# Attention outputs of a linear-attention and two-layer MoE kernel: products of 128 rows against products of 64 rows in two halves of the array

## The chip, the cores and the metric

The kernel runs on one core of a Trainium2 chip. The metric is the device time of one execution in microseconds (us), smaller is better; several executions of each kernel are timed and the median is given. The core has a matrix engine (TensorE, in the profile PE for products and PEld for the loads of their stationary operand), VectorE (DVE), ScalarE (ACT), GpSimd (POOL) and SyncE (SP), which issues most of the transfers. Products write to PSUM, eight banks of 512 fp32 values in each of 128 partitions; ACT and DVE read them from there.

## The reference

Linear attention without a softmax over 8 batches, 8 heads, 576 tokens and a head size of 64, a norm over each head, and then two layers with 512 inputs, 2048 hidden units and 512 outputs over all 4608 tokens. All in fp32.

```python
kv = einsum('bhsd,bhse->bhde', k, v)              # one 64x64 matrix for each batch and head
out = einsum('bhsd,bhde->bhse', q, kv)
rms = sqrt(mean(out * out, axis=-1, keepdims=True) + 1e-06)
x = (out / rms * g_norm)                          # then (batch, token, head * 64 + e): 4608 x 512
h = x @ moe_w_in;  y = (h * sigmoid(h)) @ moe_w_out
h2 = y @ moe2_w_in; r = maximum(h2, 0); result = (s * r * r + b) @ moe2_w_out
```

## The kernel before

The tokens of a batch are cut into four tiles of 128 tokens and a rest of 64; the rests of two neighbouring batches share one tile of 128 partitions. That makes 32 full tiles and 4 rest tiles. Batch 0 is done at the start, by itself (the last part of the code); the seven others are spread over the first layer.

The first layer runs in 7 blocks of 512 tokens with 16 slots each, one slot for 128 of the hidden units. In a slot, `emit_h` (L493) issues twelve products of 128x128 by 128x512 into a bank `ph`, and ACT applies Silu. After it, `attend` (L560) issues what the list `UNITS` assigns to this slot: for a batch b, one tile of attention in each of four or five consecutive slots, and four to eight slots later the transposes of the normed tiles. The code issues in this order by hand (a manual schedule), so that on each engine the order of the code is the order of execution. The remaining layers (the classes Hidden and Output, seven products in place of eight by Strassen's and Winograd's scheme) follow and are not touched.

One tile of attention consists of these steps:

- `emit_qT` (L373), one slot earlier: four transposes of 128x128 on PE, from q into a PSUM bank `pq`, and one ACT copy of 128x512 into `qT`, which is a part of the tile `at_kvw`. There is one such room for all tiles.
- `out_tile` (L436) calls `emit_out` (L382): for each of the four pairs of heads one fp32 product, with 128 rows (two heads of 64), the transposed q of 128 tokens as stationary operand and a 128x128 matrix `kvw` as moving operand. `kvw` holds the two heads' 64x64 matrices on its diagonal and zeros elsewhere, so that one product gives both heads. All four pairs go to one PSUM bank `po`. A rest tile has two products for each pair, one for each batch, of 64 tokens each: the left and the right half of the array's columns. An fp32 product has two records of a load and two of a matmul in the trace.
- ACT squares `po` into `sq` (L395), DVE sums the squares of each head (L396), and ACT copies `po` to `xnp` or `xr` (L444). Later DVE makes the reciprocal roots (`rsqrt_steps`), multiplies (`emit_norm`, L432), and PE transposes (`emit_xT`, L464).

The banks: `pq` and `po` take turns in the two banks a_0 and a_1. `ph` has h_0 and h_1; `pkv` (the 64x64 matrices of a batch, L353 and L359) y0; the transposes `px` y2 and y3; y1 is not used beside the first layer. In the opening of batch 0, four banks y0 to y3 hold one tile each (`pss`, L1214); for pairs 0 and 1, and then for pair 2 and pair 3, the `kv` matrices and the outputs of all four tiles are made in turn, as k and v arrive, and squares, sums, norm and transposes go tile by tile.

Of the kernel before, what the change touches and what calls it, by code (L numbers as in the profile page):

```python
# [8 lines left out]
F32 = mybir.dt.float32  # L9
F32R = mybir.dt.float32r  # L10
I32 = mybir.dt.int32
AF = mybir.ActivationFunctionType
ALU = mybir.AluOpType
AX = mybir.AxisListType
# [3 lines left out]
def kernel(  # L18
# [36 lines left out]
    nc = tc.nc  # L55
    P = 128
    B, H, S, D = q.shape
    NT, DM = out.shape
    DFF = moe_w_in.shape[1]
    NP = H // 2  # L60
    KT = DM // P
    MT = DFF // P
    T = 512
    NB = NT // T
    TT = T // P
# [19 lines left out]
    ps_y = Turns(psum, 1)  # L85
# [3 lines left out]
    def room(tag, shape, dtype, name):  # L89
        return sbuf.tile(shape, dtype, tag=tag, name=name)  # L90

    def bank(tag, name):
        return psum.tile([P, T], F32, tag=tag, name=name)
# [5 lines left out]
    def pair(tag, name):  # L99

        return room(tag, [P, 2, T], F32, name)
# [4 lines left out]
    xn_pages = [pair(tag, f"xnp{i}") for i, tag in enumerate(("XA", "XB"))]  # L106
    kvw = [at_kvw[:, 1].rearrange("p (a t) -> p a t", a=NP), const.tile([P, NP, P], F32, tag="kvw1", name="kvw1")]
# [6 lines left out]
    def runs(t):  # L114
        b, c = t
        return [(0, P, b)] if c < TT else [(i * ST, ST, b - 1 + i) for i in range(2)]
# [18 lines left out]
    def load_raw(stage, i, tag):  # L135
        a = room(tag, [P, WN, 2], I32, f"wr{stage}_{i}")
        w = weights[stage].bitcast(I32)
        if stage % 2:
            nc.sync.dma_start(
                a.rearrange("p (c f) o -> p c (f o)", c=KT),  # L140
                w[:, 4 * i * P:4 * (i + 1) * P].rearrange("(c p) f -> p c f", p=P),
            )
        else:
            nc.sync.dma_start(
                a.rearrange("p (r e) o -> p r (e o)", r=2),
                w[2 * i * P:2 * (i + 1) * P, :].rearrange("(r p) e -> p r e", p=P),
            )
        raw_t[stage, i] = a
# [178 lines left out]
    qT_t = {}  # L327
    xn_t = {}
# [43 lines left out]

    def emit_qT(t):  # L373
        a = q_t.pop(t).rearrange("p h d -> p (h d)")
        ps = ps_a.tile([P, T], F32, tag="a", name=f"pq{t[0]}_{t[1]}")
        for p in range(NP):
            nc.tensor.transpose(ps[:, p * P:(p + 1) * P], a[:, p * P:(p + 1) * P], ident)  # L377
        qT = at_kvw[:, 0].rearrange("p (a t) -> p a t", a=NP)
        nc.scalar.copy(qT.rearrange("p a t -> p (a t)"), ps)
        qT_t[t] = qT  # L380

    def emit_out(t, ps, pairs):  # L382

        po = ps.rearrange("p h d -> p (h d)")
        for p in pairs:
            for off, n, b in runs(t):
                nc.tensor.matmul(  # L387
                    po[off:off + n, p * P:(p + 1) * P], qT_t[t][:, p, off:off + n], kvw[b % 2][:, p, :],
                    start=True, stop=True,
                )  # L390

    def emit_squares(t, ps, ms):

        sq = work.tile([P, H, D], F32, tag="sg", name=f"sq{t[0]}_{t[1]}", bufs=3)
        nc.scalar.activation(sq, ps, AF.Square)  # L395
        nc.vector.reduce_sum(ms, sq, axis=AX.X)  # L396

    def rsqrt_steps(r, tiles):
# [24 lines left out]
    def xn_page(t):  # L423
        if t[1] == TT:
            return room("gl_0", [P, H, D], F32, f"xr{t[0]}")
        return xn_pages[t[1] // 2][:, t[1] % 2].rearrange("p (h d) -> p h d", h=H)

    def emit_norm(t, x, y):
        xn = xn_t.get(t)
        if xn is None:  # L430
            xn = xn_t[t] = xn_page(t)
        nc.vector.tensor_tensor(xn, x, y.rearrange("p (h o) -> p h o", o=1).to_broadcast([P, H, D]), op=ALU.mult)  # L432

    r_t = {}

    def out_tile(t):  # L436
        b, i = t
        if i == 0:
            r_t[b] = small.tile([P, 4, 6 * H], F32, tag="r", name=f"r{b}", bufs=1)
        ps = ps_a.tile([P, H, D], F32, tag="a", name=f"po{b}_{i}")  # L440
        emit_out(t, ps, range(NP))
        emit_squares(t, ps, r_t[b][:, 0, i * H:(i + 1) * H])
        xn_t[t] = xn_page(t)
        nc.scalar.copy(xn_t[t], ps)  # L444

    def norm_tile(t):
        b, i = t
# [89 lines left out]
    def first_load_q(i):  # L537
        a = spare(f"W{5 + i}", f"q0_{i}").rearrange("p (h c d) -> p h c d", h=NP, c=TT)
        x = q[0, i * NP:(i + 1) * NP, :T, :]
        nc.sync.dma_start(a.rearrange("p h c d -> p h (c d)"), x.rearrange("h (p c) d -> p h (c d)", c=TT))  # L540
        return a
# [477 lines left out]
    def warm_up(n):  # L1019

        ps = ps_h.tile([P, T], F32, tag="h", name="warm")
        for _ in range(n):
            nc.tensor.matmul(ps, kvw[1][:, 0, :], kvw[1].rearrange("p a t -> p (a t)"), start=True, stop=True)
# [162 lines left out]
    with tc.manual_schedule():  # L1186
        load_raw(1, 0, "wr_0")
        qs = [first_load_q(0), first_load_q(1)]
        kvs = [first_load_kv(0), first_load_kv(1)]
        kvz = first_load_z()  # L1190
        load_raw(1, 1, "wr_1")
        kvs += [first_load_kv(2), first_load_kv(3)]
        nc.vector.memset(bcol, 0.0)
        nc.vector.memset(ones, 1.0)
        nc.scalar.activation(scol, bcol, AF.Silu)
        for t in kvw:
            nc.gpsimd.memset(t, 0.0)
        make_identity(nc, ident)
        gv = g_norm.rearrange("(d o) -> d o", o=1)
        for i in range(2):  # L1200
            nc.scalar.dma_start(gcol[i * D:(i + 1) * D], gv)
        nc.scalar.dma_start(scol, moe2_s.rearrange("(a o) -> a o", o=1).to_broadcast([P, 1]))
        nc.scalar.dma_start(bcol, moe2_b.rearrange("(a o) -> a o", o=1).to_broadcast([P, 1]))
        warm_up(4)

        def first_kv(p):
            a = kvs[p]
            kv_t[0, p] = []
            for i in range(2):
                kv_t[0, p] += [a[:, i], [kvz[:ST, i, 2 * p + h] for h in range(2)]]  # L1210
            emit_kv(0, [p])

        r = r_t[0] = small.tile([P, 4, 6 * H], F32, tag="r", name="r0", bufs=1)
        pss = [ps_y.tile([P, H, D], F32, tag=f"y{t}", name=f"po{t}") for t in range(TT)]  # L1214
        decode_first(0, "rebias", "low", "sign", "merge")
        decode_first(0, "high", "rest")
        for t in range(TT):
            first_qT(t, qs)
        first_kv(0)
        first_kv(1)  # L1220
        for t in range(TT):
            emit_out((0, t), pss[t], (0, 1))
        decode_first(1, "rebias", "low", "sign", "merge")
        load_kv(1, 0)
        load_kv(1, 1)
        for p in (2, 3):
            first_kv(p)
            for t in range(TT):
                emit_out((0, t), pss[t], (p,))
            load_kv(1, p)  # L1230
        for t in range(TT):
            emit_squares((0, t), pss[t], r[:, 0, t * H:(t + 1) * H])
        decode_first(1, "high")
        warm_up(4)
        for step in rsqrt_steps(r, range(TT)):
            step()
        for t in range(TT):
            emit_norm((0, t), pss[t], r[:, 2, t * H:(t + 1) * H])
        for t in range(TT):
            if t < 2:  # L1240
                emit_xT((0, t), ps_a.tile([P, NP, P], F32, tag="a", name=f"px0_{t}"))
            else:
                emit_xT((0, t), ps_y.tile([P, NP, P], F32, tag=f"y{t - 2}", name=f"px{t}"))
        decode_first(1, "rest")
        decode_first(2, "rebias", "low", "sign", "merge")

        def in_spares():

            kept = {}

            def granule(n):
                if n % 2 == 0:
                    kept[0] = room(SPARES[n // 2 % NA], [P, 2, 2, 2 * P], F32R, f"wo{n}")
                return kept[0][:, n % 2]

            return granule

        def in_pages(n):
            return room(("kvw1_0", "gh_0", "v_0")[n % 3], [P, 2, 2 * P], F32R, f"wp{n}")

        steps = (f for s in (
            weight_steps(2, ("wr_0", "wr_1"), ("v_0", "v_1"), in_spares(), 3, behind=3),
            weight_steps(3, ("wr_0", "wr_1"), ("v_0", "v_1"), in_spares(), 3),
        ) for f in s)
        steps4 = weight_steps(4, ("wr_1",), ("K",), in_pages, 2)
        for j in range(PB):
            for m in range(MT):
                emit_h(j, m)
                first_stage(j, m, steps)
        hidden1.run(beside1)  # L1270
        out2.run(beside2)
        hidden3.run(beside3)
        do_some(steps4, 1000)
        out4.run(beside4)
# [33 lines left out]
```

## Time and profile before

| | |
|---|---|
| median of 3 executions | 1563.76 us (1562.29 to 1566.73) |
| the profiled execution's own time | 1564.93 us |
| its span in the profile | 1562.8 us |
| PE busy | 1541.8 us, 99% of the span |
| DVE busy | 1016.7 us, 65% |
| ACT busy | 821.5 us, 53% |
| granted TensorE clock | 1.0 |

A profile shows each engine's instructions with start and duration. Busy time is the union of these durations; for PE they overlap, since a matmul's record runs from its start to the end of its pipeline, so that the step from one start to the next tells the cost in a sequence, not the record's duration. The chain of waits follows the work that ended last back through what released it, and merges what follows without a gap into one piece.

### The profile page before, as it was taken

How to read it: one execution, taken by the hardware profiler on the slowest of the kernel's cores; microseconds unless marked ns; L12 is line 12 of the kernel's file. 1: busy time of each engine (PE TensorE's matmuls, PEld its weight loads, DVE VectorE, ACT ScalarE, POOL GpSimd, SP SyncE). 2: the span in 40 equal slices, each digit the busy share in tenths (PEclk: the TensorE clock that was granted, in tenths of full speed). 3: DMA queues.
4: the chain of work that ended last, by engine and by line, in shares of the span. 5: the costliest groups of instructions: out<-in, count | busy, mean ns of one | idle time of the engine just before them, and what ended most of it. 6: DMA issues, size and time to landing. Idle time of an engine off the chain costs nothing.

```text
span 1562.8 us, 21817 instructions
## 1 busy us (share of the span) xinstructions
PE 1541.8 (99%) x8184; PEld 1296.0 (83%) x8184; DVE 1016.7 (65%) x1435; ACT 821.5 (53%) x1311; POOL 1.6 (0%) x8
## 2 busy tenths in 40 slices
PE   7999999999999999999999999999999999999998
PEld 4888888888888888888988788888889888888888
DVE  5655466557674868676776666766646767575845
ACT  4655545555465444444545565656555454545454
POOL 0000000000000000000000000000000000000000
PEclk9999999999999999999999999999999999999999
DMA  7988798877665882724767756475577782726233
GB/s 256 300 276 279 266 300 283 298 262 258 253 224 208 337 308 83 251 78 143 241 251 309 277 197 250 166 262 187 202 268 271 291 300 70 242 72 239 80 108 109
DMA packets 228969, 353.77 MB, mean 226 GB/s; under 512 B 56576, under 2 KB 97024, under 8 KB 228864
## 3 DMA queue, kind: packets, MB, share of 16 engines
q1 hardware_dynamic: 163968, 243.83, 46.4%
q10 hardware_dynamic: 64896, 108.55, 18.5%
q8 instruction: 64, 1.05, 0.3%
q14 instruction: 41, 0.34, 0.1%
HBM read 211.81 MB, written 140.51 MB: 225 GB/s over the span
## 4 chain that ended last, share of the span: by engine, by line
PE 94%; DMA 2%; ACT 1%; DVE 1%; issue 0%; SPq 0%; ACTq 0%; DVEq 0%
PE ph L500 19%; PE qy L991 19%; PE qx L991 12%; PE qv L991 12%; PE py L721 11%; PE px L721 7%; PE pv L721 7%; PE po L387 2%; PE pkv L353 1%; PE px L464 1%; PE pt L918 1%; PE pq L377 1%; DMA wd<-wp 1%; DMA kv<-in_v_dram 1%; DMA kvz<-in_v_dram 1%; DMA sa<-gt 0%
## 5 line engine op out<-in xcount | busy, mean ns | idle before, releaser
L991 PE MATMUL qy<-o,w 128*128 128x512 f32 (+1 forms) x1440 | 299.4, 368 | 0.8 <-DVE o L878 0.8
L991 PEld LDWEIGHTS qy<-o,w 128*128 128x128 f32 x1440 | 251.2, 188 | 46.0 <-DVE o L878 1.0
L878 DVE TENSOR_TENSOR o<-ka,o 128x1024 fp32r<-128x1024 f32 (+1 forms) x160 | 178.6, 1117 | 103.2 <-ACT o L876 98.7
L876 ACT CAST o<-ka 128x1024 fp32r<-128x1024 f32 (+1 forms) x160 | 154.5, 967 | 167.1 <-PE qv L991 74.2
L991 PE MATMUL qv<-o,w 128*128 128x512 f32 (+1 forms) x960 | 202.9, 369 | 0.0
L991 PE MATMUL qx<-o,w 128*128 128x512 f32 (+1 forms) x960 | 202.8, 369 | 0.0
L991 PEld LDWEIGHTS qx<-o,w 128*128 128x128 f32 x960 | 167.1, 189 | 29.6
L991 PEld LDWEIGHTS qv<-o,w 128*128 128x128 f32 x960 | 167.0, 189 | 29.4
L721 PE MATMUL py<-x,w 128*128 128x512 f32 (+1 forms) x720 | 161.8, 369 | 4.0 <-ACT g L758 4.0
L721 PEld LDWEIGHTS py<-x,w 128*128 128x128 f32 x720 | 126.4, 189 | 27.8 <-ACT g L758 4.8
L507 ACT ACTIVATE g<-ph 128x512 f32<-128x512 f32 x112 | 66.9, 598 | 145.8 <-PE ph L500 141.4
L500 PE MATMUL ph<-xh,wh 128*128 128x512 f32 x448 | 127.6, 406 | 0.8 <-ACT xh L468 0.8
L876 ACT CAST o<-r 128x1024 fp32r<-128x1024 f32 (+1 forms) x80 | 77.3, 966 | 83.7 <-PE qy L991 42.8
L500 PE MATMUL ph<-xl,wh 128*128 128x512 f32 x448 | 120.5, 391 | 0.0
L500 PE MATMUL ph<-xh,wl 128*128 128x512 f32 x448 | 120.4, 390 | 0.0
L878 DVE TENSOR_TENSOR o<-r,o 128x1024 fp32r<-128x1024 f32 (+1 forms) x80 | 89.4, 1118 | 37.4 <-ACT o L876 36.7
L721 PE MATMUL pv<-x,w 128*128 128x512 f32 (+1 forms) x480 | 111.6, 368 | 0.0
L721 PE MATMUL px<-x,w 128*128 128x512 f32 (+1 forms) x480 | 111.5, 368 | 0.0
L500 PEld LDWEIGHTS ph<-xl,wh 128*128 128x128 f32 x448 | 84.0, 188 | 18.9 <-DVE xl L469 0.4
L500 PEld LDWEIGHTS ph<-xh,wl 128*128 128x128 f32 x448 | 84.1, 188 | 18.6
L721 PEld LDWEIGHTS px<-x,w 128*128 128x128 f32 x480 | 84.9, 189 | 15.1
L721 PEld LDWEIGHTS pv<-x,w 128*128 128x128 f32 x480 | 84.7, 189 | 14.9
(162 smaller groups left out, 1868.6 us busy)
## 6 DMA issues: line engine op xcount, KB each, us to landing
r<-gt SPq DMA_DIRECT2D x96, 512.0 KB, 4.6
gt<-g ACTq DMA_DIRECT2D x176, 256.0 KB, 2.3
w<-wd SPq DMA_DIRECT2D x84, 512.0 KB, 7.1
gt<-g ACTq DMA_DIRECT2D x56, 512.0 KB, 4.6
wd<-wo SPq DMA_DIRECT2D x112, 256.0 KB, 4.3
wr<-in_moe_w_in_dram SPq DMA_DIRECT2D x16, 1024.0 KB, 6.0
wr<-in_moe_w_out_dram SPq DMA_DIRECT2D x16, 1024.0 KB, 5.9
ka<-gt SPq DMA_DIRECT2D x32, 512.0 KB, 3.7
```

The costliest lines, as they stand in the source:

```text
L353: nc.tensor.matmul(ps[r, p, r], ka[:, i, d], va[:, i, d], start=(p == pairs[0] and c == 0), stop=False, skip_group_check=True,)
L377: nc.tensor.transpose(ps[:, p * P:(p + 1) * P], a[:, p * P:(p + 1) * P], ident)
L387: nc.tensor.matmul(po[off:off + n, p * P:(p + 1) * P], qT_t[t][:, p, off:off + n], kvw[b % 2][:, p, :], start=True, stop=True,)
L464: nc.tensor.transpose(ps[:, p, :], xn[:, p * P:(p + 1) * P], ident)
L500: nc.tensor.matmul(ps, wt[:, c, :], xt[:, c, :], start=(n == 0 and c == 0), stop=(n == 2 and c == KT - 1))
L507: nc.scalar.activation(both[:, i], ps, AF.Silu)
L721: nc.tensor.matmul(ps, a[s][c], x[t][c], start=(k in (P1, P5) and n == c == 0), stop=(n == 2 and c == 1), skip_group_check=True,)
L876: nc.scalar.copy(o[:, :, 0], x)
L878: nc.vector.tensor_sub(o[:, :, 1], x, o[:, :, 0])
L918: nc.tensor.transpose(ps[:, e * P:(e + 1) * P], self.c[b, h, e][:, r * P:(r + 1) * P], ident)
L991: nc.tensor.matmul(ps, t[:, s], self.o[u][:, i, p], start=(k in (P1, P5) and a == i == m == 0), stop=(a == NA - 1 and i == 1 and m == 2), ...
```

## The change

The output products are made for each head by itself. For each pair of heads, the even head's product takes the upper 64 rows of the array (partitions 0 to 63 of `qT` and of `kvw`) and the odd head's the lower 64 rows, with 64 columns of `kvw` as moving operand in place of 128. Even heads go to one PSUM bank and odd heads to another: a_0 and a_1 in the first layer. So there are twice as many products, each with half the rows and half the moving columns; the stationary operand has 128 tokens as before (64 in a rest tile). `pq` moves to the bank y1. ACT copies the two banks into the two interleaved halves of `xnp` (two copies of 128x256), and squares `xnp` from there and not from PSUM. In the opening, a bank holds the even or the odd heads of two tiles; squares, sums and norm go bank by bank, in the same number and size, with the tiles' heads taken by stride.

```diff
--- before.py
+++ after.py
@@ -372,27 +372,29 @@
 
     def emit_qT(t):
         a = q_t.pop(t).rearrange("p h d -> p (h d)")
-        ps = ps_a.tile([P, T], F32, tag="a", name=f"pq{t[0]}_{t[1]}")
+        ps = bank("y1_0", f"pq{t[0]}_{t[1]}")
         for p in range(NP):
             nc.tensor.transpose(ps[:, p * P:(p + 1) * P], a[:, p * P:(p + 1) * P], ident)
         qT = at_kvw[:, 0].rearrange("p (a t) -> p a t", a=NP)
         nc.scalar.copy(qT.rearrange("p a t -> p (a t)"), ps)
         qT_t[t] = qT
 
-    def emit_out(t, ps, pairs):
-
-        po = ps.rearrange("p h d -> p (h d)")
+    ROWS = [slice(i * D, (i + 1) * D) for i in range(2)]
+
+    def emit_out(t, banks, pairs):
+
         for p in pairs:
-            for off, n, b in runs(t):
-                nc.tensor.matmul(
-                    po[off:off + n, p * P:(p + 1) * P], qT_t[t][:, p, off:off + n], kvw[b % 2][:, p, :],
-                    start=True, stop=True,
-                )
-
-    def emit_squares(t, ps, ms):
+            for i, r in enumerate(ROWS):
+                for off, n, b in runs(t):
+                    nc.tensor.matmul(
+                        banks[i][off:off + n, p, :], qT_t[t][r, p, off:off + n], kvw[b % 2][r, p, r],
+                        start=True, stop=True,
+                    )
+
+    def emit_squares(t, x, ms):
 
         sq = work.tile([P, H, D], F32, tag="sg", name=f"sq{t[0]}_{t[1]}", bufs=3)
-        nc.scalar.activation(sq, ps, AF.Square)
+        nc.scalar.activation(sq, x, AF.Square)
         nc.vector.reduce_sum(ms, sq, axis=AX.X)
 
     def rsqrt_steps(r, tiles):
@@ -426,9 +428,7 @@
         return xn_pages[t[1] // 2][:, t[1] % 2].rearrange("p (h d) -> p h d", h=H)
 
     def emit_norm(t, x, y):
-        xn = xn_t.get(t)
-        if xn is None:
-            xn = xn_t[t] = xn_page(t)
+        xn = xn_t[t]
         nc.vector.tensor_tensor(xn, x, y.rearrange("p (h o) -> p h o", o=1).to_broadcast([P, H, D]), op=ALU.mult)
 
     r_t = {}
@@ -437,11 +437,12 @@
         b, i = t
         if i == 0:
             r_t[b] = small.tile([P, 4, 6 * H], F32, tag="r", name=f"r{b}", bufs=1)
-        ps = ps_a.tile([P, H, D], F32, tag="a", name=f"po{b}_{i}")
-        emit_out(t, ps, range(NP))
-        emit_squares(t, ps, r_t[b][:, 0, i * H:(i + 1) * H])
-        xn_t[t] = xn_page(t)
-        nc.scalar.copy(xn_t[t], ps)
+        banks = [bank(f"a_{n}", f"po{b}_{i}_{n}").rearrange("p (h d) -> p h d", d=D)[:, :NP] for n in range(2)]
+        emit_out(t, banks, range(NP))
+        x = xn_t[t] = xn_page(t)
+        for n in range(2):
+            nc.scalar.copy(x[:, n::2], banks[n])
+        emit_squares(t, x, r_t[b][:, 0, i * H:(i + 1) * H])
 
     def norm_tile(t):
         b, i = t
@@ -1211,31 +1212,45 @@
             emit_kv(0, [p])
 
         r = r_t[0] = small.tile([P, 4, 6 * H], F32, tag="r", name="r0", bufs=1)
-        pss = [ps_y.tile([P, H, D], F32, tag=f"y{t}", name=f"po{t}") for t in range(TT)]
+        pss = [ps_y.tile([P, 2, NP, D], F32, tag=f"y{n}", name=f"po{n}") for n in range(TT)]
+
+        def first_out(p):
+            for t in range(TT):
+                emit_out((0, t), [pss[t // 2 * 2 + i][:, t % 2] for i in range(2)], (p,))
+
+        def of_bank(x, n):
+            t = n // 2 * 2
+            return x.rearrange("p (t a i) -> p t a i", t=TT, i=2)[:, t:t + 2, :, n % 2]
+
         decode_first(0, "rebias", "low", "sign", "merge")
         decode_first(0, "high", "rest")
         for t in range(TT):
             first_qT(t, qs)
         first_kv(0)
         first_kv(1)
-        for t in range(TT):
-            emit_out((0, t), pss[t], (0, 1))
+        for p in (0, 1):
+            first_out(p)
         decode_first(1, "rebias", "low", "sign", "merge")
         load_kv(1, 0)
         load_kv(1, 1)
         for p in (2, 3):
             first_kv(p)
-            for t in range(TT):
-                emit_out((0, t), pss[t], (p,))
+            first_out(p)
             load_kv(1, p)
-        for t in range(TT):
-            emit_squares((0, t), pss[t], r[:, 0, t * H:(t + 1) * H])
+        for n in range(TT):
+            sq = work.tile([P, 2, NP, D], F32, tag="sg", name=f"sq0_{n}", bufs=3)
+            nc.scalar.activation(sq, pss[n], AF.Square)
+            nc.vector.reduce_sum(of_bank(r[:, 0, :TT * H], n), sq, axis=AX.X)
         decode_first(1, "high")
         warm_up(4)
         for step in rsqrt_steps(r, range(TT)):
             step()
         for t in range(TT):
-            emit_norm((0, t), pss[t], r[:, 2, t * H:(t + 1) * H])
+            xn_t[0, t] = xn_page((0, t))
+        for n in range(TT):
+            to = xn_pages[n // 2].rearrange("p t (a i d) -> p t a i d", a=NP, i=2)[:, :, :, n % 2]
+            y = of_bank(r[:, 2, :TT * H], n).rearrange("p t (a o) -> p t a o", o=1)
+            nc.vector.tensor_tensor(to, pss[n], y.to_broadcast([P, 2, NP, D]), op=ALU.mult)
         for t in range(TT):
             if t < 2:
                 emit_xT((0, t), ps_a.tile([P, NP, P], F32, tag="a", name=f"px0_{t}"))
```

## Rows read from the trace of the kernel before

**Rows 1.** The page: engines' busy time; lines of the chain that ended last

```profile
PE 1541.8 (99%) x8184; PEld 1296.0 (83%) x8184; DVE 1016.7 (65%) x1435; ACT 821.5 (53%) x1311; POOL 1.6 (0%) x8
...
PE ph L500 19%; PE qy L991 19%; PE qx L991 12%; PE qv L991 12%; PE py L721 11%; PE px L721 7%; PE pv L721 7%; PE po L387 2%; PE pkv L353 1%; PE px L464 1%; PE pt L918 1%; PE pq L377 1%; DMA wd<-wp 1%; DMA kv<-in_v_dram 1%; DMA kvz<-in_v_dram 1%; DMA sa<-gt 0%
```

**Rows 2.** Windows: stretch, its length, each engine's busy time, clock

```profile
core 0: us, PE busy (x) PEld busy (x) DVE busy (x) ACT busy (x) POOL busy (x), PEclk, DMA share, GB/s
...
80.00:380.00 300.00, 300.00 (x1969) 252.46 (x1967) 175.33 (x402) 161.60 (x322) 0.00 (x0) 1.00 0.84 279
```

**Rows 3.** The chain in order of time, 238 to 337 us: start, length, what

```profile
238.05 0.89 PE po L387 x8
238.94 0.44 PE pq L377 x4
239.38 2.77 PE ph L500 x12
...
246.25 1.02 PE po L387 x16
247.27 8.38 PE ph L500 x36
...
298.23 0.89 PE po L387 x8
299.12 10.90 PE ph L500 x48
...
331.03 2.02 PE pkv L353 x64
333.05 0.61 PE pkv L359 x16
333.66 2.97 PE ph L500 x12
```

**Rows 4.** Timeline inside a rest tile, 150 us: start, length, engine, what

```profile
150.11 0.27 PE L387 MATMUL po<-at_kvw 128*64 128x128 f32 x1
...
150.12 0.27 PE L387 MATMUL po<-kvw,at_kvw 128*64 128x128 f32 x1
...
150.22 0.27 PE L387 MATMUL po<-at_kvw 128*64 128x128 f32 x1
...
150.33 0.27 PE L387 MATMUL po<-at_kvw 128*64 128x128 f32 x1
```

**Rows 5.** Matmuls by line: ns min/median/max, rows*columns of the stationary operand

```profile
L387 PE MATMUL po<-kvw,at_kvw x160: 270/275/377, 52.3 to 357.0; 128*128 128x128 f32 x128, 128*64 128x128 f32 x32
...
L387 PE MATMUL po<-at_kvw x8: 272/273/323, 150.0 to 150.8; 128*64 128x128 f32 x8
...
L353 PE MATMUL pkv<-kv x64: 222/222/270, 166.2 to 168.1; 128*64 128x64 f32 x64
...
L359 PE MATMUL pkv<-kvz x16: 218/218/267, 168.2 to 168.7; 64*64 64x64 f32 x16
...
L464 PE MATMUL px<-ident,xnp x128: 270/272/329, 31.7 to 375.5; 128*128 128x128 f32 x128
```

**Rows 6.** ACT: copies of two sizes, and one tile's ACT work

```profile
L444 ACT COPY xnp<-po x28: 581/582/592, 55.5 to 353.6; 128x512 f32<-128x512 f32 x28
...
L758 ACT COPY g<-py 128x256 f32<-128x256 f32 x8 | 2.8, 354 | 0.0
...
234.88 0.60 ACT L395 ACTIVATE sq<-po 128x512 f32<-128x512 f32 x1 [0.29 <-PE po L387]
235.37 0.58 ACT L444 COPY xnp<-po 128x512 f32<-128x512 f32 x1
235.83 0.61 ACT L379 COPY at_kvw<-pq 128x512 f32<-128x512 f32 x1
```

**Rows 7.** The opening's chain and timeline, 24 to 36 us

```profile
24.55 1.16 PE L387 MATMUL po<-at_kvw,qT 128*128 128x128 f32 x8 [0.52 <-ACT at_kvw L361]
25.08 2.06 ACT L395 ACTIVATE sq<-po 128x512 f32<-128x512 f32 x4 [0.58 <-PE po L387]
...
30.96 2.48 DVE L432 TENSOR_TENSOR xnp<-po,r 128x512 f32<-128x512 f32 x4
31.71 2.45 PE L464 MATMUL px<-ident,xnp 128*128 128x128 f32 x16 [2.57 <-DVE xnp L432]
32.41 2.48 ACT L468 ACTIVATE xh<-px,cols 128x512 fp32r<-128x512 f32 x4 [4.34 <-PE px L464]
...
34.94 1.21 PE L500 MATMUL ph<-xh,wh 128*128 128x512 f32 x4 [0.78 <-ACT xh L468]
```

**Rows 8.** The chain beside batch 1's tiles, 56 to 66 us

```profile
56.60 1.16 PE po L387 x8
...
64.57 0.50 ACT at_kvw L379
65.11 1.16 PE po L387 x8
```

## The prediction

> **What bounds the kernel now.** I read the page first. PE is busy for 99% of the span and stands for nearly all of the chain that ended last; of the changed lines, `po` has 2% of that chain, some 31 us, and `pq` 1% [rows 1]. The windows come next: from 80 to 380 us, where six of the seven spread batches run, PE is busy for all 300.00 us at the full clock, and DVE and ACT for little more than half [rows 2]. There, each nanosecond by which PE's sequence grows or shrinks moves the end. So the question is what one tile costs in PE's sequence, and for that the chain in order of time serves: a full tile takes 0.89 us, eight records at 0.111 us, four transposes follow in 0.44, and then twelve `ph` matmuls in 2.77 [rows 3].
>
> **What the array does with smaller products.** The trace has no product of 64 rows by 128 columns, but three neighbours of one. The first is the rest tile, whose stationary operands are 128 rows by 64 columns, in two column halves. Its two halves start together, and the next pair 0.11 us later, and so on [rows 4]: two halves run at the same time, each with its own load and its own moving columns. Sixteen records go in eight steps of 0.109, 0.87 us, but the row says 1.02 [rows 3]; so 0.15 is lost at the entry. The exit costs too: 36 `ph` matmuls after it take 8.38 us, where 48 after a full tile take 10.90, 0.227 each; 36 would be 8.18, so 0.20 is lost. The second and third neighbours say the same: `pkv` (128*64) and `pkvz` (64*64) run in pairs, and the `ph` behind them take 2.97 in place of 2.77, again 0.20 [rows 3]. `pkv` with an entry of 0.15 has 32 pairs in 1.87 us, 0.058 each; `pkvz` has eight pairs, 0.47 at that step, and takes 0.61: going from 128*64 to 64*64, rows alone, costs 0.14 as well.
>
> The first matmul after an entry or a wait lasts longer than its like, because its load is not hidden [rows 5]: with 128 columns by 377 - 275 = 102 ns, with 64 columns by 323 - 273 = 50, in `pkv` by 270 - 222 = 48, in `pkvz` by 267 - 218 = 49. So a load takes the time of its columns, and 64 rows load no faster than 128. Taken from the 0.15 and 0.20, these leave about 0.10 us at each entry and each exit in which the array empties. For transposes the exposed load is 329 - 272 = 57 ns.
>
> **The change part by part.** The moving columns are halved, but not the columns that are loaded: each of the 16 records of a full tile still loads 128, some 0.10 to 0.11 us. If the two row halves load and multiply side by side, as column halves do in [rows 4], each half does eight loads one after another, at the old step of 0.11, and the matmul of 64 columns (0.055, half of 0.11) hides under the next load. Halving the products gains nothing, then, and each full tile gets an entry and an exit of its own:
>
> - entry: 0.10 empty + 0.10 exposed load = 0.20
> - from the first to the last product: 7 x 0.11 = 0.77
> - the last product's own columns: 0.055
> - exit to the transposes `pq`: 0.10 + 0.057 = 0.16; where no `pq` follows (the last tile of a batch with four), exit to `ph`: 0.20
>
> That is 1.185 us, or 1.225, against 0.89: 0.295 or 0.335 more. Of the 28 full tiles beside the first layer, batches 2 to 7 have 24, of which 21 are followed by `pq` and 3 by `ph`: 21 x 0.295 + 3 x 0.335 = **7.2 us**. The bounds: with nothing lost in emptying, 2 x 0.10 x 24 = 4.8 less; with loads at 0.102, 0.06 x 24 = 1.4 less; with the loads of both halves one after another, 8 x 0.109 = 0.87 more for each tile (a rival below).
>
> On the loads the Trainium skill goes further than these rows. "TensorE: Matmul & The Clock Gate", section "LDWEIGHTS (loading the stationary operand)", has the time by columns over 1.2 GHz whatever the rows; an estimate from it is 107 ns for each of the new loads, and the sum would be the same. The exposed loads in [rows 5] agree for 64 columns; no row has 64 rows with 128 columns.
>
> The four rest tiles are divided already, so entry and exit stay. They become 32 records in four quarters of 64*64, whose step is 0.058 where two run at once: 8 x 0.058 = 0.47 if four do, 0.93 if two do, against 0.87. Three of them are on PE's path: -1.2 to +0.2, and I take **-0.5**, between the two, since the rows show two at once and exclude nothing of four.
>
> Batch 1's four full tiles lie where PE twice waits for ACT's `qT` copy (the tile's piece is 1.16 and not 0.89, after the copy) [rows 8]. Each wait already contains an exposed load and some 0.2 us of idle time, which cover the entry and more there. 4 x 0.295 = 1.2, of which I let two tiles be covered: **+0.6**, between 0 and 1.2.
>
> ACT: one copy of 128x512, 582 ns, becomes two of 128x256, for which the nearest row is 354 each, so 0.13 us more for a tile [rows 6]; the square has the same size. It delays the `qT` copy by as much. That copy ends at 236.4 in [rows 6], and the tile that needs it starts at 238.05 [rows 3], so 1.6 us cover it; without that cover it would cost 0.13 x 28 = 3.6. The two banks a_0 and a_1 must both be free before the next tile, but ACT empties them before it copies `qT`, for which that tile waits anyway; `pq` has y1 to itself. DVE's sum comes 0.13 us later, and the norm slots later. Taken at nothing.
>
> The opening: four output products of the last pair, then ACT's squares from 25.08, DVE's sums and roots, the four norms from 30.96, transposes from 31.71, ACT's four `xh` from 32.41, and the first `ph` at 34.94 [rows 7]. It is a chain, and the new order lengthens it twice. The first square needs a bank that two tiles share, so it waits for two tiles more records: 2 x 0.11 = 0.22. The first transpose needs the even and the odd bank, so two norms in place of one: 2.48 / 4 = 0.62. Sum 0.84. Entry and exit stand there already, since 64*64 products are ahead. **+0.85**, between 0.2 and 1.5.
>
> Sum: 7.2 - 0.5 + 0.6 + 0.85 = 8.15 us. The profiled execution took 1564.93 us (its span and 2.1 outside), 1.17 above the median of 1563.76; so 1573.1 beside that execution, and **1572** beside the median.
>
> **The rivals.**
>
> *The halves load in turn.* If the loads of upper and lower half share one path, a full tile has 16 x 0.109 in a row: 0.87 more than above, 24 x 0.87 = 20.9; batch 1 some 3, the opening 1.7 (8 records more for pair 2 and 8 for pair 3), the rests 0.5. 8.15 + 26.1 = 34 more: **1597**. For it: no row shows two row halves at all. Against it: column halves have loads and matmuls of their own [rows 4]. "TensorEngine Tiling (Array Packing)" in the Trainium skill, "Key Properties", says that different tiles load and multiply in parallel; the rows bear this out for column halves.
>
> *A load is not hidden under its own half's matmul.* Then the step is 0.11 + 0.055: 8 x 0.055 x 24 = 10.6 more, **1583**. Against it: the column halves hide theirs.
>
> *Half-height loads are fast.* If the step is that of `pkv`, 0.058, the tile is 0.15 + 7 x 0.058 + 0.055 + 0.16 = 0.77: 0.12 less than before, 21 x 0.12 + 3 x 0.08 = 2.8 less, and with the opening and rests the time is about **1561**, no change that can be told.
>
> *Faster:* the same, and row halves need no emptying. Then it is 0.57 a tile, 0.32 x 24 = 7.7 less: **1556**. It decides from a tile of about 0.69 us (4.7 / 24 below 0.89); with the 0.37 of entry, last product and exit as measured, the step would have to be under 0.05. Against it: 64*64 loads are exposed for 49 ns, as 128*64 ones, and a change of rows alone costs 0.14. The Trainium skill's table "Theoretical Speedup" ("TensorEngine Tiling (Array Packing)") has up to twice the speed at 64; by it 28 x 0.445 = 12.5 less, 1551; no row here shows that for loads of 128 columns.
>
> **How the numbers follow.** What this kernel's measurement can tell from no change is about 0.3%, 4.7 us. The forecast (1566 to 1577 by its bounds: half the emptying gone, or both doubtful covers missing and 1 us of scatter) gets 0.71; loads in turn 0.13; loads not hidden 0.04; fast loads, same time, 0.07; faster 0.05. Slower by over 0.3% is over 1568.5: most of the first (0.64), and the next two, 0.81. Same: 0.07 and the first one's low end 0.07, 0.14. Faster 0.05. The range takes the first whole, the third, and of the loads in turn what lies under 1599: 1565 to 1599.
>
> **What the profile will show.** A full tile as 16 `po` records of 64*128 shape, its two halves starting together, each half's step near 0.11 and not 0.058; the piece in the chain near 1.0, and `ph` behind a batch's last tile 0.2 longer; the first record of a tile and the first `pq` long by an exposed load. The window from 80 on is still full of PE. Rests shorter than 1.02 only if four quarters run at once. The first `ph` near 35.8. A step of 0.22 would show loads in turn, one of 0.058 that load time falls with the rows; either would make me wrong, as would a tile that follows `ph` without a gap.

## The result and the profile after

| | before | after |
|---|---|---|
| median | 1564.67 us (4 executions) | 1574.49 us (1571.56 to 1575.54, 4 executions) |
| ratio | 1 | 1.0055, 95% interval 1.0042 to 1.0068 |
| span of the profiled execution | 1562.8 us | 1573.1 us |
| granted clock in it | 1.0 | 0.997 |

The change makes the kernel slower by 0.55%, 8.6 us by the ratio. The forecast was 1572, slower, with a range of 1565 to 1599.

The page after, busy time: PE has 320 more matmuls and 10.3 us more, as much as the span has grown; DVE has the same, ACT 6 us more.

```profile
PE 1552.1 (99%) x8504; PEld 1297.4 (82%) x8504; DVE 1016.6 (65%) x1435; ACT 827.2 (53%) x1343; POOL 1.6 (0%) x8
```

The chain in order of time (start, length, what), to be held against [rows 3]:

```profile
156.08 0.62 PE po L389 x32
156.71 8.39 PE ph L501 x36
...
236.71 1.04 PE po L389 x16
237.75 0.58 PE pq L377 x4
238.34 2.76 PE ph L501 x12
...
254.23 0.64 PE po L389 x32
...
307.37 1.04 PE po L389 x16
308.41 11.12 PE ph L501 x48
```

A full tile takes 1.04 where it took 0.89, and the transposes behind it 0.58 where they took 0.44: 1.62 against 1.33, 0.29 more. Where `ph` follows, 48 of them take 11.12 against 10.90, so that 0.37 is added there in all. The rest tile, 32 records in four quarters, is shorter: 0.62 in batch 3 (156.08) against 1.02, 0.40 less, and the 36 `ph` behind it take 8.39 as they took 8.38. In batch 5 (254.23) a wait follows it.

The matmuls of single lines (duration ns min/median/max) in two stretches, of full tiles, of a rest tile and of the transposes:

```profile
L389 PE MATMUL po<-at_kvw x64: 272/272/320, 102.7 to 116.6; 64*128 64x64 f32 x64
...
L389 PE MATMUL po<-at_kvw x16: 218/218/267, 156.0 to 156.5; 64*64 64x64 f32 x16
...
L377 PE MATMUL pq<-ident,qp x12: 272/273/328, 103.7 to 112.8; 128*128 128x128 f32 x12
```

The same 64 moving columns take 218 ns in a quarter and 272 in a half: each matmul of a full tile waits 54 ns for its load, which has twice as many columns (the first experiment tests this reading). The first one waits 320 - 218 = 102 ns, the load of 128 columns with nothing beside it. The first transpose waits 328 - 273 = 55.

Three waits are on the path: before the first `ph`, before batch 1's first `px` and before batch 5's. Their rows in the timeline, with the opening's first output products above them (start, length, engine, what, and in brackets the idle time before it and what ended it); then batch 1's first `px` in the kernel before:

```profile
22.05 2.19 PE L389 MATMUL po<-at_kvw,qT 64*128 64x64 f32 x16 [0.30 <-ACT at_kvw L361]
...
37.59 1.21 PE L501 MATMUL ph<-xh,wh 128*128 128x512 f32 x4 [0.92 <-ACT xh L469]
...
83.26 0.66 PE L465 MATMUL px<-ident,xnp 128*128 128x128 f32 x4 [1.78 <-DVE xnp L432]
...
263.73 0.66 PE L465 MATMUL px<-ident,xnp 128*128 128x128 f32 x4 [0.49 <-DVE xnp L432]
```

```profile
79.56 0.66 PE L464 MATMUL px<-ident,xnp 128*128 128x128 f32 x4 [0.68 <-DVE xnp L432]
```

The first `ph` comes at 37.59 where it came at 34.94 [rows 7], 2.65 later. Batch 1's first `px` comes at 83.26; it came at 79.56, with a wait of 0.68: 3.70 later. Batch 5's had no such wait. From there the account of the profiled executions closes: 3.70 up to 83 us; 21 x 0.28 + 3 x 0.36 = 6.96 for the full tiles of batches 2 to 7; 3 x 0.40 = 1.2 less for their rest tiles; 0.7 for the wait at 263.7 (0.49, and 0.2 by which the first `px` is longer). That makes 10.2 at the end of the attention, and the spans differ by 10.3. This is more than the ratio's 8.6, and part of it is the granted clock: a half (1.2 of 2.4 GHz) from 20.6 to 30.8 us in this execution, full in that of the kernel before.

### The profile page after: what moved, and what is told of

Its sections match the earlier page's. It is cut to its first block, busy times and chain, and to the rows that moved or that the text cites. A ratio compares the mean times of both kernels' runs of the same rounds, so it can differ in the third digit from the quotient of the medians.

```text
span 1573.1 us, 22455 instructions
## 1 busy us (share of the span) xinstructions
PE 1552.1 (99%) x8504; PEld 1297.4 (82%) x8504; DVE 1016.6 (65%) x1435; ACT 827.2 (53%) x1343; POOL 1.6 (0%) x8
## 4 chain that ended last, share of the span: by engine, by line
PE 93%; DMA 2%; DVE 2%; ACT 1%; issue 1%; SPq 0%; ACTq 0%; DVEq 0%
PE qy L992 19%; PE ph L501 19%; PE qx L992 12%; PE qv L992 12%; PE py L722 11%; PE px L722 7%; PE pv L722 7%; PE po L389 2%; PE pq L377 1%; PE pkv L353 1%; PE px L465 1%; PE pt L919 1%; DMA q<-in_q_dram 1%; DMA wd<-wp 1%; DMA kv<-in_v_dram 1%
```

## The experiments

The theory: each full tile enters and leaves the 64-row division of the array, where the array empties and a load is exposed, and within it the step is that of a 128-column load, so that halving the moving columns gains nothing. The rivals: the step of 0.11 is two matmuls of 0.055 in turn; the divided records are slower in themselves and a switch is free; the loss comes from ACT's and DVE's new order; or it comes from the opening. Diffs are against the changed kernel. The four executions of the changed kernel span 4 us, so where an experiment has one execution, its chain tells more than its time.

**Twice the moving columns.** Beside the first layer only:

```diff
-  banks[i][off:off + n, p, :], qT_t[t][r, p, off:off + n], kvw[b % 2][r, p, r],
+  banks[i][off:off + n, p, :], qT_t[t][r, p, off:off + n], kvw[b % 2][r, p, :] if t[0] else kvw[b % 2][r, p, r],
...
-  nc.scalar.copy(x[:, n::2], banks[n])
+  nc.scalar.copy(x[:, n::2], banks[n][:, :, ROWS[n]])
```

> Beside the first layer, each product of 64 rows gets 128 moving columns in place of 64 (the head's own 64 and the zeros beside them); loads and switches as in the changed kernel. Theory (the step of 0.11 us is that of a 128-column load, and both row halves multiply at once): a full tile's step stays at 0.11, its piece in the chain goes from 1.04 to about 1.09 (the last product is longer), the rest tile, whose loads are short, goes from 0.62 to about 1.0; in all 2 to 3 us more than the changed kernel, about 1577. Rival (the loads are fast, and the 0.11 are two matmuls of 0.055 in turn, one for each half): the step goes to 0.22, a tile costs 0.8 more, and the time is 1594 or more.

Measured: 1578.63 us in one execution. The chain, and the durations by line:

```profile
237.87 1.09 PE po L389 x16
238.96 0.58 PE pq L377 x4
```

```profile
L389 PE MATMUL po<-kvw,at_kvw x80: 269/272/373, 237.8 to 256.4; 64*128 64x128 f32 x64, 64*64 64x128 f32 x16
```

Twice the multiplication costs a full tile 0.05 us. The matmuls of 128 moving columns last 272 ns, as those of 64 did: the 54 ns of waiting for the load are now filled with multiplying. That the half itself isn't slower shows in the rest tile, whose quarters take 269 ns for the same 128 columns. So the loads set the step, and both halves multiply at the same time. The time is 1.6 above what was expected; in this execution the clock was a half from 33.2 to 40 us.

**Half the columns in each load.** The 128 tokens of a stationary operand are cut in two, in the opening too:

```diff
+  def halves_of(t):
+      return [(i * ST, ST, t[0]) for i in range(2)] if t[1] < TT else runs(t)
...
-  for off, n, b in runs(t):
+  for off, n, b in halves_of(t):
```

> Each load of 128 tokens is cut into two of 64 tokens, in the left and right half of the array's columns, so that a full tile is 32 records in four quarters of 64 by 64, as the rest tile already is. Theory (loads bind): the step is 0.058, a full tile's piece is 0.62 in place of 1.04, as the rest tile's, so 24 x 0.41 = 10 us less than the changed kernel: 1564 to 1566, about the time of the kernel before. Rival (matmuls or the PSUM banks bind, or the number of records): the step for the same work stays at 0.11 or grows, and the time is 1574 or more.

Measured: 1564.36 us (10 executions), ratio to the kernel before 0.9993, interval 0.9982 to 1.0003. The chain and the durations:

```profile
237.26 0.62 PE po L392 x32
237.88 0.59 PE pq L377 x4
```

```profile
L392 PE MATMUL po<-kvw,at_kvw x144: 218/218/267, 229.3 to 245.6; 64*64 64x64 f32 x144
```

Twice the records, and the tile goes from 1.04 to 0.62; no matmul but the first waits for its load any more (218 ns). The loss of the change is gone, with its switches, its new ACT order and the opening's order of banks still there.

**Full rows, 64 moving columns.** The products of one head each, in the same banks, but with all 128 rows:

```diff
-  qT_t[t][r, p, off:off + n], kvw[b % 2][r, p, r],
+  qT_t[t][r if t[0] == 0 else slice(0, P), p, off:off + n],
+  kvw[b % 2][r if t[0] == 0 else slice(0, P), p, r],
```

> Beside the first layer, the two products of a pair of heads are made with all 128 rows (the other head's rows meet zeros in `kvw`) and 64 moving columns, into the same two banks as in the changed kernel: as many records, loads and moving columns, but no division of the array for full tiles. Theory (the two row halves load at the same time, which is what the division gives, and the switches are what it costs): the loads stand one after another, 16 steps of 0.11 and no entry or exit, so the piece of a full tile goes from 1.04 to about 1.78, and from the last `ph` to the first transpose 0.87 - 0.28 = 0.6 more; the rest tiles go from 0.62 to about 1.02; in all 24 x 0.6 + 3 x 0.4 = 15 to 18 us more than the changed kernel, 1590. Rival (the halves of the changed kernel load in turn as well, or the loads are fast): no more than the changed kernel, 1574 or less.

Measured: 1591.17 us in one execution. The chain:

```profile
245.73 1.73 PE po L389 x16
247.46 0.44 PE pq L377 x4
```

Sixteen loads in a row, at 0.108 each, and no entry or exit: the first `po` starts 228 ns after the last `ph`, as in the kernel before (318 in the changed kernel), and the transposes are back at 0.44, though `po` and `pq` alternate as before. So the division does let two loads run at once, and it saves 0.55 us a tile (2.17 against 1.62) over products of one head without it. It is the doubling of the loads that it does not pay for.

**Two more switches for a tile.** Only the order changes:

```diff
-  emit_out(t, banks, range(NP))
+  emit_out(t, banks, (0, 1))
+  pq = half_qT((b, i + 1)) if i + 1 < n_tiles else None    # two of the next tile's four transposes
+  emit_out(t, banks, (2, 3))
```

> The same products in another order: two pairs of heads, two of the next tile's transposes, the other two pairs, the other two transposes, so that a tile that is followed by transposes enters and leaves the 64-row division twice and not once. Theory (each entry costs 0.09 empty and 0.10 exposed load, each exit 0.09 and 0.057): 0.34 a tile, 21 to 25 tiles, 7 to 8.5 us more than the changed kernel, 1581 to 1583. Rival (changing the division costs nothing, the 64-row records are slower in themselves): no change, 1574.

Measured: 1582.11 us in one execution. The chain:

```profile
240.04 0.59 PE po L399 x8
240.63 0.37 PE pq L379 x2
```

The two halves of a tile now take 2 x (0.59 + 0.37) = 1.92 against 1.62: 0.30 for a pair of switches with the same records. Over 25 tiles that is 7.5 us; the time is 7.6 above the changed kernel's median. The price is that of a switch, since the same alternation without a division costs nothing (0.44 for the transposes in the experiment above). The Trainium skill has the rule: "TensorEngine Tiling (Array Packing)", section "Key Properties", says that a change of the tiling mode, not just of the tile, drains the engine. The trace agrees, with 0.09 us empty at an entry (the first `po` starts 318 ns after the last `ph` and not 228) and 0.09 at the exit (the first transpose starts 202 ns after the last `po` and not 111), besides the exposed loads.

**Squares before copies.**

```diff
-  for n in range(2):
-      nc.scalar.copy(x[:, n::2], banks[n])
-  emit_squares(t, x, r_t[b][:, 0, i * H:(i + 1) * H])
+  sq = work.tile([P, H, D], F32, tag="sg", name=f"sq{t[0]}_{t[1]}", bufs=3)
+  for n in range(2):
+      nc.scalar.activation(sq[:, n::2], banks[n], AF.Square)
+  nc.vector.reduce_sum(r_t[b][:, 0, i * H:(i + 1) * H], sq, axis=AX.X)
+  for n in range(2):
+      nc.scalar.copy(x[:, n::2], banks[n])
```

> ACT squares both banks from PSUM before it copies them, as the kernel before did with its one bank; the changed kernel copies first. Theory: DVE's sum of a rest tile came 0.7 us later after the banks were ready, since the square stands behind two copies, and with it came the rest of DVE's queue, so that PE waits for the norm at 83.3 us (1.78) and at 263.7 (0.49); with the squares first these waits shrink by 0.5 to 0.7 us each, 1.0 to 1.3 us in all. Rival (these waits come from PE's and the transfers' other times): they stay within 0.2.

Measured: 1572.75 us in one execution. First the changed kernel's timeline of the rest tile of batch 5, then the kernel before's of the same tile, then this one's of batch 1's `px` and its chain behind batch 5's rest tile:

```profile
254.89 0.65 ACT L444 COPY xr<-po 128x256 f32<-128x256 f32 x2
255.57 0.63 ACT L397 ACTIVATE sq<-xr 128x512 f32<-128x512 f32 x1
...
256.24 0.69 DVE L398 TENSOR_REDUCE r<-sq 128x8 f32<-128x512 f32 x1 [2.07 <-ACT sq L397]
```

```profile
247.32 0.60 ACT L395 ACTIVATE sq<-po 128x512 f32<-128x512 f32 x1 [0.44 <-PE po L387]
...
247.95 0.69 DVE L396 TENSOR_REDUCE r<-sq 128x8 f32<-128x512 f32 x1 [2.34 <-ACT sq L395]
```

```profile
80.68 0.66 PE L468 MATMUL px<-ident,xnp 128*128 128x128 f32 x4 [1.10 <-DVE xnp L432]
```

```profile
252.32 8.39 PE ph L504 x36
260.71 0.49 PE px L468 x4
```

In the changed kernel the sum starts 1.35 us after ACT begins with the tile, since the square stands behind two copies; in the kernel before it was 0.63 (square at 247.32, sum at 247.95). With the squares first the wait of 1.78 is 1.10, and that of 0.49 is gone (`px` follows `ph` at 260.71): 1.2 us. The time, 1.7 below the changed kernel's median but above its lowest, can't show this by itself. That the first `ph` came earlier here, at 35.73, is not the reason: in the next experiment, with the copies first, it comes at 34.80 and batch 1's wait is 1.75.

**The opening of before.** The opening's products, banks, squares and norm as in the kernel before, the rest as changed:

```diff
-  pss = [ps_y.tile([P, 2, NP, D], F32, tag=f"y{n}", name=f"po{n}") for n in range(TT)]
+  pss = [ps_y.tile([P, H, D], F32, tag=f"y{t}", name=f"po{t}") for t in range(TT)]
...
+  emit_out128((0, t), pss[t], (p,))      # 128 rows, 128 moving columns, as before
```

> The opening of batch 0 as in the kernel before (128 rows, one bank for a tile), the seven other batches as in the changed kernel. Theory: the opening costs 2.65 us, since the first matmul of the first layer comes at 37.6 and not at 34.9 us; all of it is on the path, so 2.6 less than the changed kernel, about 1572, and the clock stays at 1.0 in the opening. Rival (batch 1 waits for ACT and DVE anyway, which covers the opening's loss): less than 1 us.

Measured: 1573.23 us (4 executions), ratio 1.0052, interval 1.0038 to 1.0066. It can't be told from the changed kernel's 1.0055. But the two intervals together leave some 3 us either way, so the times neither confirm the expected 2.6 nor exclude it. In its profile, at a clock of 1.00, the first `ph` comes at 34.80 and batch 1's first `px` at 80.69, 2.57 earlier than in the changed kernel's: batch 1 doesn't cover what the opening loses, and the rival is excluded for this pair of executions.

**A filled gap.** `warm_up(2)`, two idle products of 128x512, behind the outputs of pairs 0 and 1:

```diff
   for p in (0, 1):
       first_out(p)
+  warm_up(2)
```

> The changed kernel with two more idle products of 128x512 after the outputs of pairs 0 and 1, where PE waits for k and v. Theory: the granted clock was 0.5 from 20.6 to 30.8 us, which the kernel before does not have; with the gap filled it stays at 1.0, and the first matmul of the first layer comes at about 35.8 (0.85 after that of the kernel before, by the order of banks alone), 1.8 less than in the changed kernel. Rival (the low clock lies beside waits for k, v, ACT and DVE): the first matmul stays near 37.6.

Measured: 1574.84 us in one execution; the first `ph` at 36.28, between the two. Busy time by windows (stretch, length, PE, PEld, DVE, ACT, POOL, clock, DMA), of the kernel after and of the first experiment, whose opening is the same:

```profile
20.00:31.00 11.00, 10.04 (x76) 7.69 (x77) 5.16 (x10) 3.82 (x9) 0.00 (x0) 0.53 0.97 288
```

```profile
20.00:31.00 11.00, 8.11 (x80) 5.29 (x80) 7.50 (x20) 3.82 (x9) 0.00 (x0) 1.00 0.95 285
```

The same opening has a clock of 0.53 in this stretch in one execution and 1.00 in another, without the filler; so the filler's 1.00 proves nothing. In the first experiment the clock fell later, to a half from 33.2 us, so its 35.37 is not that of a full clock either.

What the order of banks costs shows where the clocks agree, counted from the third pair's first `pkv` to the first `ph`. The kernel before and this experiment had the full clock in all of this stretch:

```profile
20.52 0.69 PE L353 MATMUL pkv<-kv 128*64 128x64 f32 x16 [1.78 <-DMA kv<-in_v_dram]
...
34.94 1.21 PE L500 MATMUL ph<-xh,wh 128*128 128x512 f32 x4 [0.78 <-ACT xh L468]
```

```profile
21.37 0.69 PE L353 MATMUL pkv<-kv 128*64 128x64 f32 x16
...
36.28 1.21 PE L501 MATMUL ph<-xh,wh 128*128 128x512 f32 x4 [0.92 <-ACT xh L469]
```

That is 14.42 and 14.91 us, 0.49 more. The squares-first experiment (new opening) and the last one below (old opening) both had a half clock from about 32 to 35 us:

```profile
19.86 0.69 PE L353 MATMUL pkv<-kv 128*64 128x64 f32 x16 [0.30 <-DMA kv<-in_v_dram]
...
35.73 1.21 PE L504 MATMUL ph<-xh,wh 128*128 128x512 f32 x4 [0.78 <-ACT xh L472]
```

```profile
19.71 0.69 PE L353 MATMUL pkv<-kv 128*64 128x64 f32 x16
...
35.09 1.21 PE L521 MATMUL ph<-xh,wh 128*128 128x512 f32 x4 [0.78 <-ACT xh L489]
```

That is 15.87 and 15.38, again 0.49. The profiled execution of the changed kernel takes 17.23 from 20.36, 2.81 more than the kernel before, so some 2.3 us of its delay go with the low clock.

**A version for both.** Quarters in the seven batches, squares first, the opening of the kernel before (its code is that of the three experiments above):

> Quarters of 64 by 64 in the seven batches, squares before copies, and the opening of the kernel before. Theory: from the rest tile's records a full tile with its switches takes 1.00 us from the last `ph` to the first transpose, where the kernel before takes 1.12: 21 x 0.12 + 3 x 0.07 = 2.7 and some 0.4 in batch 1, so 3 us less than the kernel before, 1561 to 1562, a ratio of 0.998. Rival (ACT's two copies and two squares in place of one of each, or the switches, take it back): 1564 or more.

Measured: 1561.42 us (11 executions), ratio 0.9981, interval 0.9972 to 0.9990, so 3.0 us less than the kernel before. The chain:

```profile
243.40 0.62 PE po L392 x32
244.03 8.39 PE ph L521 x36
252.42 0.48 PE px L485 x4
252.90 2.74 PE ph L521 x12
```

`px` follows `ph` without a wait here. With 0.62 and 0.59 in place of 0.89 and 0.44 a tile gains 0.12 on the kernel before. The expectation left out that the three rest tiles gain as well. By the starts of the same `ph` in the two traces, the lead is 4.6 us at the end of the attention: 2.8 for the full tiles of batches 2 to 7, 1.2 for the rest tiles, 0.6 before them. This execution is the fastest of the eleven; the 3.0 of the ratio (1.6 to 4.4 by its interval) is the figure to keep, and that it equals the expected 3 is in part luck.

## Why the prediction was right, step by step

**Loads set the step.** Right, and shown three ways: doubling the matmul costs 0.05 a tile, halving the load's columns takes 0.42 off, and the durations differ by the load. Inside a full tile the step is 0.11 as forecast. A load of 64 rows and 128 columns was a gap in the rows of before; it is exposed for 102 ns. "TensorE: Matmul & The Clock Gate" of the Trainium skill, section "LDWEIGHTS (loading the stationary operand)", by columns alone, gives 107 as an estimate, and the trace agrees within 5 ns.

**Two halves load at once.** Right; the version without the division has 1.73 in place of 1.04. With it falls the rival of loads in turn (whose sum, 8.15 + 26.1, gives 1598 and not 1597; nothing hangs on it), and the piece of 1.04 also excludes that a load is not hidden under its own half's matmul.

**Entry and exit.** Right: 1.185 was forecast and 0.295 more, with `ph` behind 0.335 more; the trace has 0.28 to 0.29 and 0.36. 7.2 us was forecast for batches 2 to 7, and it is 7.0. Batch 1's four full tiles, +0.6 in the forecast, also came out: PE's delay against the kernel before grows from 2.41 (`ph` at 52.14 and 49.73) to 3.01 (69.72 and 66.71), 0.30 at each of two tiles and next to nothing at the two that waited for ACT before.

**The rest tiles.** I took -0.5, between two quarters at once and four. Four run at once: 3 x 0.40 = -1.2, the end of the range that was given.

**ACT and DVE "taken at nothing".** This term was mis-sized. I counted 0.13 us for two copies in place of one and overlooked that the square had moved behind them, so that the sum came 0.72 later and not 0.13. DVE's queue behind it (steps of the weights' decoding, the roots, the norm) came late with it. What was "slots later" in the code was close in time: batch 1's `px` already waited before, and batch 5's had no 0.5 us to spare. Batch 1's wait grew by 1.10, of which its rest tile's gain covers 0.4, and batch 5 lost 0.7: 1.4 us where nothing was counted. Squaring first takes back 1.2 by the waits.

**The opening.** 0.85 was forecast for the order of banks, between 0.2 and 1.5; where the clocks agree it is 0.49. The profiled execution has 2.65, most of it for the clock, of which the prediction had no term. That belongs to the account of the two profiles. The ratio can't tell: putting back the old opening changed it by 0.0003, within both intervals.

The sum was 8.15 and the ratio says 8.6. With the terms as measured and the clock left aside it is 7.0 - 1.2 + 0.6 + 1.4 + 0.5 = 8.3. That the total fits so well is in part luck: 1.4 us that were taken at nothing are made up by the rest tiles (0.7), the opening (0.35) and the full tiles (0.2), each of which came out lower than forecast.

**Left open:** what lets the clock fall in the opening in some executions and not in others. It is not the new opening alone. With the old one it fell to a half from 10.8 to 14.2 and from 31.3 to 34.7 us in the last version's profile, and of the 15 executions of the kernel before that were timed beside the last three experiments above, 13 have a mean clock of 0.996 to 0.999. The two at 1.000 took 1562.79 and 1563.92 us, the three at 0.996 1565.59 to 1568.82. In the changed kernel's profile PE had been busy for 6.88 of the 10 us from 10 to 20 when the clock fell at 20.6; in the first experiment's for 6.90, and there it kept the full clock until 33.2. The runs don't isolate it.

## What to carry to other kernels

Count loads, not only products: here, where the loads set the step, a product gained only from a cut along the columns of the stationary operand; cutting rows and moving columns left each load as long as it was and doubled their number. A division of the array is entered and left, some 0.3 us for a pair here, so it must save more than that in one visit. When a step moves from PSUM to a copy in SBUF, it also moves behind the copy, and everything that waits for it moves too. And look at the granted clock of both profiles before a difference between them is put down to the change.

## What I had not expected of the hardware

Four quarters of 64 by 64 run at once, with loads and matmuls of their own: 32 records in 0.62 us, entry included, where 16 records in two column halves take 1.02 [rows 3].

A matmul's record here begins before its own load is done: 272 ns in place of 218 for the same 64 moving columns, where 128 columns take 272 and 269. So the wait for a load shows in the duration, not as a gap.
